# Another order and other engines for attention pairs 0 to 17, weights' sums in halves, part of the norms on VectorE, biases as immediates

## The chip, the cores and the metric

The kernel runs on one core of a Trainium2 chip. The metric is the device time in microseconds of that core, as the median of several runs. Engines are named as in the profile: PE (TensorE, matmuls), DVE (VectorE), ACT (ScalarE), POOL (GpSimd), SP (SyncE, which here only issues DMAs).

## The reference

`q`, `k`, `v` are [8 batches, 12 heads, 448 positions, 64 dimensions] in float32. The result is [3584, 768].

```python
q_n = q / (np.linalg.norm(q, axis=-1, keepdims=True) + 1e-06)
k_n = k / (np.linalg.norm(k, axis=-1, keepdims=True) + 1e-06)
attn = softmax(q_n @ k_n.T / tau)                  # per batch and head, tau = 0.1
x = (attn @ v) with heads side by side             # [3584, 768]
h = x @ w_in                                       # [3584, 2048]
g = h * np.clip(h + 3.0, 0.0, 6.0) / 6.0
out = g @ w_out                                    # [3584, 768]
```

## The kernel before

Two heads make a pair, 48 pairs in all, six to a batch; two pairs make a twin, whose raw `q` and `k` are items `2d` and `2d + 1`. An item is loaded (LQ, two 448 KB tiles of 128 x 896 columns), squared (SQ, on ACT, DVE or POOL, in pieces of columns of 64 if wanted; `SQ.6.v.1.3` is item 6 on DVE, 3 columns from the first), summed (RE, DVE), its reciprocal norms are made (NO: four small ACT operations Ln, Exp, Ln with bias EPS, Exp), and it is normalised (NM, POOL or DVE, into bf16). Then it is transposed: on PE through the identity (TR) for items 0 to 13, by a DMA transpose (XD) from item 14 on. CQ and CK copy a pair's queries and keys out of the transposed tile, CS the last keys; `km` is a copy by POOL for those that came by DMA. For each pair there are four groups of scores (SC), their exponentials (EX, ACT), the products with the values (VA, PE), and the division by the sums (FI, DVE: reciprocal L477, product L478). VC casts the values. BK and CX transpose the result and copy it into `xT`; XP and XB do that by DMA.

When a batch is complete, its MoE units run: 16 `mm1_unit`s (six matmuls, then a relu on ACT, L577, then the product with the bank on DVE, L583, into `gT`), and for batch 0 six `mm2_unit`s (16 matmuls, L615, and a store copied alternately by ACT and DVE). From pair 18 on the second layer uses a scheme with fewer matmuls for blocks of 2 x 2, which needs sums of parts of `w_out` (WS: "1", "6", "7" into `w_sum`, "y3" and "y4" in place; 3072 columns each, L690) and of `gT` (`g_sum`, L719). Outputs of units and scores share a ring of six PSUM banks; before pair 6 scores use two double banks of their own.

Every engine executes its own instructions in the order in which the program issues them, and waits for semaphores of the others. That order is written out by hand: for pairs 0 to 17 in the list `PLAN` (611 tokens, each one step; `U` issues the next MoE unit's matmuls, `UA` and `UV` the oldest outstanding step of a unit on ACT and DVE), and for the rest in loops. `DP.n` and `D.n` are `n` filler matmuls on zeros (`busy_pv`, L923, and `busy`, L918), which compute nothing that is used. `W` lets POOL issue a DMA of one eighth of the weights. `LV` loads a twin's values with four DMAs.

Of the kernel before, what the change touches and what calls it, by code (L numbers as in the profile page):

```python
# [14 lines left out]
EPS = 1e-6  # L15
# [3 lines left out]
ORDER = "111111111111111111111111111111222222"  # L19

PLAN = [
# [36 lines left out]
]  # L58


# [1 line left out]
def kernel(  # L62
# [83 lines left out]
        [const.tile([128, 2, 14], FP32, name=f"{x}{i}", tag=f"{x}{i}") for x in ("ln", "nr", "le", "r")]  # L146
        for i in range(2)
    ]
    bias = const.tile([128, 2], FP32, name="bias", tag="bias")
    eps_bias, half_bias = bias[:, 0:1], bias[:, 1:2]  # L150
    ident = const.tile([128, 128], BF16, name="ident", tag="ident")

    PV = psum.tile([128, 2, 512], FP32, name="PV", tag="PV")
# [92 lines left out]
    def norms(d, *items):  # L246

        needs(("NM", 2 * d - 4), ("NM", 2 * d - 3))
        items = items or (0, 1)
        for x in items:  # L250
            needs(("RE", 2 * d + x))
        it = slice(items[0], items[-1] + 1)
        ln, nr, le, r = (t[:, it, :] for t in rs[d % 2])
        nc.scalar.activation(out=ln, in_=n2s[d % 2][:, it, :], func=AF.Ln)
        nc.scalar.activation(out=nr, in_=ln, func=AF.Exp, scale=0.5)
        nc.scalar.activation(out=le, in_=nr, func=AF.Ln, bias=eps_bias)
        nc.scalar.activation(out=r, in_=le, func=AF.Exp, scale=-1.0)  # L257
        for x in items:
            issued.add(("NO", d, x))

# [301 lines left out]
    def mm1_unit(b, fc):  # L562
# [12 lines left out]
        def relu():  # L575
            u = sb.tile([128, S], BF16, name="u", tag="u", bufs=3)
            nc.scalar.activation(  # L577
                out=u[:, :], in_=ps[:, 0:S], func=AF.Relu, bias=half_bias, scale=1.0 / 6.0
            )
            post["v"].append(lambda: product(u))  # L580

# [90 lines left out]
            return wide[n % 2], wide[2]  # L672
        return wide_late[2 * (n - LOOP) : 2 * (n - LOOP) + 2]

    def weight_sums(what, c0, n):

        w = w_out_sb[:, :, :].rearrange("p (c k) m -> p c k m", k=2)[:, c0 : c0 + n]
        b11, b12, b21, b22 = (w[:, :, k, m] for k in range(2) for m in (LEFT, RIGHT))
        for x in {"y3": "16", "y4": "17"}.get(what, ""):
            assert all((x, c) in summed for c in range(c0, c0 + n))  # L680
        o, x, y, op = {
            "1": (b11, b11, b22, ALU.add),
            "6": (b11, b11, b12, ALU.add),
            "7": (b21, b21, b22, ALU.add),
            "y3": (b12, b12, b22, ALU.subtract),
            "y4": (b21, b21, b11, ALU.subtract),
        }[what]
        if what in w_sum:
            o = w_sum[what][:, c0 : c0 + n, :]
        nc.vector.tensor_tensor(out=o, in0=x, in1=y, op=op)  # L690
        summed.update((what, c) for c in range(c0, c0 + n))

    def half(b, t, k):
# [247 lines left out]
    def whole_units(n, engines="av"):  # L941
# [4 lines left out]
                    finish_units(e)  # L946

    OPS = {
        "LQ": load_qk, "LV": load_v, "W": next_weights, "SQ": square, "RE": reduce, "NO": norms,
        "NM": normalise, "VC": vcast, "TR": transposes, "XD": crossbar, "XB": back_crossbar, "XP": back_two, "CQ": copy_q, "CK": copy_k, "CS": copy_k3, "SC": scores,  # L950
        "EX": exps, "VA": values, "FI": finish_values, "BK": back, "CX": copy_x, "U": unit, "UA": lambda: finish_units("a"), "UV": lambda: finish_units("v"),
        "GL": g_left, "WS": lambda x, *h: weight_sums(str(x), *((h[0] * KC // 2, KC // 2) if h else (0, KC))), "UU": whole_units, "D": busy, "DP": busy_pv, "OPEN": open_ring,
    }

    def do(op, *args):
        OPS[op](*args)
        key = (op,) + tuple(a for a in args if isinstance(a, int))
        if op not in ("RE", "NM", "LQ"):
            issued.add(key[:3] if op == "SC" else key)

    def run(text):
# [7 lines left out]
        nc.vector.memset(t[0:64, 2:4, 0, :], 0.0)  # L969
    zeros = xT[1][:, 0, :]  # L970
    nc.vector.memset(zeros, 0.0)
    nc.vector.memset(eps_bias, EPS)
    nc.vector.memset(half_bias, 0.5)
    make_identity(nc, ident)
    for t in vx:
        nc.vector.memset(t[:, :, D : D + 1], 1.0)
# [120 lines left out]
```

## Time and profile before

| | |
|---|---|
| runs | 405.06, 405.01, 406.67 us; median 405.06 |
| span of the profiled execution (first to last instruction) | 405.6 us; its time outside the span is not recorded |
| granted TensorE clock, mean | 0.998 |
| busy: PE / DVE / ACT / POOL | 396.2 / 288.9 / 278.3 / 233.5 us |
| first filler matmul, first scores, first exponential, first MoE unit | 2.47, 13.66, 14.20, 44.24 us |
| DMA engines' share, 22.4 to 44.2 us | 1.11 (259 GB/s) |

PE's busy time includes fillers, and matmuls overlap, so a busy PE may still have short stalls; the spacing of starts shows them. A line of a timeline gives the start, the length, the engine, the line of the kernel, the operation, what it writes and reads, its shape and how many such instructions were merged, and in brackets the idle time before it and what ended it.

### The profile page before, as it was taken

To read this page: it belongs to the slowest core of one execution; us is meant where nothing else is said; L and a number is where in the kernel's file an instruction comes from. 1 tells how busy PE (TensorE), PEld (TensorE's weight loads), DVE (VectorE), ACT (ScalarE), POOL (GpSimd) and SP (SyncE) were. 2 spreads that over 40 slices of the span, in tenths; PEclk is the share of its full clock that TensorE was granted. 3 is DMA by queue.
4 is the path that set the end of the run, shared out by engine and by line. 5 is a ranking of instruction groups with operands and counts; after the bars stand their busy time and mean duration, and the time that the engine had idled before them with its cause. 6 is when DMAs were issued, how large, how long until landed. Compare 5 with 4: busy or idle time off the path is not lost.

```text
span 405.6 us, 9619 instructions
## 1 busy us (share of the span) xinstructions
PE 396.2 (98%) x3696; PEld 234.5 (58%) x3696; DVE 288.9 (71%) x503; ACT 278.3 (69%) x609; POOL 233.5 (58%) x228
## 2 busy tenths in 40 slices
PE   7899999999989999999999999999999999999996
PEld 4666565555655555655555556556555556555554
DVE  5888777766998777777857887587656666645663
ACT  4899998888467687687767778778757755225230
POOL 6799645761483996587475874886674600410060
PEclk9999999999999999999999999999999999999999
DMA  8899989979988749886799649977964522140134
GB/s 286 251 251 244 236 237 226 184 112 192 223 208 190 184 109 199 200 220 143 172 196 223 132 129 180 184 194 144 188 158 86 112 45 58 40 87 20 24 75 99
DMA packets 91566, 65.32 MB, mean 161 GB/s; under 512 B 56064, under 2 KB 89984, under 8 KB 91520
## 3 DMA queue, kind: packets, MB, share of 16 engines
q1 hardware_dynamic: 87408, 58.02, 62.4%
q0 software_dynamic: 3712, 6.29, 9.0%
q8 instruction: 29, 0.48, 0.5%
q10 hardware_dynamic: 400, 0.39, 0.3%
q14 instruction: 17, 0.14, 0.1%
HBM read 47.19 MB, written 11.01 MB: 143 GB/s over the span
## 4 chain that ended last, share of the span: by engine, by line
PE 91%; DVE 3%; DMA 3%; POOL 1%; SPq 1%; issue 0%; DVEq 0%; POOLq 0%
PE M L568 24%; PE M L741 17%; PE PV L457 13%; PE Y L568 6%; PE M L417 6%; PE Z L568 5%; PE Y L741 4%; PE Z L741 3%; PE M L615 3%; DMA big<-in_q_dram 3%; PE M L821 2%; PE Z L417 2%; PE Z L821 1%; PE Y L417 1%; PE PV L923 1%; PE SC L417 1%
## 5 line engine op out<-in xcount | busy, mean ns | idle before, releaser
L435 ACT ACTIVATE at<-M 128x448 bf16<-128x448 f32 x200 | 99.8, 567 | 16.4 <-PE M L417 14.3
L568 PE MATMUL M<-xT,w_in_sb 128*128 128x448 bf16 x522 | 110.7, 352 | 0.0
L568 PEld LDWEIGHTS <-w_in_sb 128*128 128x128 bf16 x768 | 71.9, 98 | 62.4 <-issue 2.5
L269 POOL TENSOR_TENSOR nrm<-big,r 128x896 bf16<-128x896 f32 (+1 forms) x48 | 79.4, 1658 | 26.0 <-ACT r L257 19.2
L577 ACT ACTIVATE u<-M,bias 128x448 bf16<-128x448 f32 x87 | 57.0, 655 | 26.0 <-PE M L568 25.5
L583 DVE SCALAR_TENSOR_TENSOR gT<-u,M 128x448 bf16<-128x448 bf16 x76 | 46.8, 618 | 38.0 <-ACT u L577 37.3
L226 POOL TENSOR_TENSOR big<-big 128x896 f32<-128x896 f32 (+3 forms) x39 | 63.4, 1628 | 10.0 <-DVE rc L477 5.1
L457 PEld LDWEIGHTS <-at 128*128 128x128 bf16 (+1 forms) x1536 | 54.8, 97 | 24.0 <-issue 14.7
L457 PE MATMUL PV<-vx,at 128*128 128x65 bf16 (+1 forms) x1536 | 64.3, 194 | 0.2 <-DVE on L478 0.2
L238 DVE TENSOR_REDUCE n<-big 128x14 f32<-128x896 f32 (+1 forms) x50 | 51.9, 1041 | 6.2 <-ACT big L224 5.5
L374 POOL COPY km<-tT 64x128 bf16<-64x128 bf16 x34 | 12.7, 372 | 59.6 <-DMA tT<-nrm 44.1
L770 POOL TENSOR_TENSOR big<-big 128x384 f32<-128x384 f32 x11 | 11.8, 1071 | 54.7 <-ACT big L789 54.6
L741 PEld LDWEIGHTS <-gT 128*128 128x128 bf16 x288 | 27.8, 98 | 20.5 <-DVE gT L719 0.8
L741 PE MATMUL M<-w_out_sb,gT 128*128 128x384 bf16 x208 | 37.9, 326 | 0.3 <-DVE gT L719 0.3
L288 POOL CAST vx<-big 128x512 bf16<-128x512 f32 x44 | 33.5, 765 | 3.5 <-DMA big<-in_v_dram 2.4
L435 ACT ACTIVATE at<-Z 128x448 bf16<-128x448 f32 x49 | 27.7, 565 | 9.9 <-PE M L417 7.1
L478 DVE TENSOR_TENSOR on<-PV,rc 128x512 bf16<-128x512 f32 x48 | 33.2, 691 | 1.7
L417 PE MATMUL M<-tT,kz 64*128 64x448 bf16 (+1 forms) x175 | 31.9, 351 | 1.0 <-DVE o L628 1.0
L741 PEld LDWEIGHTS <-gs 128*128 128x128 bf16 x224 | 21.6, 98 | 14.5
L568 PE MATMUL Y<-xT,w_in_sb 128*128 128x448 bf16 x132 | 28.6, 353 | 0.0
L435 ACT ACTIVATE at<-Y 128x448 bf16<-128x448 f32 x45 | 25.7, 570 | 3.1 <-PE Z L417 2.9
L741 PE MATMUL M<-w_sum,gs 128*128 128x384 bf16 x144 | 26.3, 326 | 0.0
(133 smaller groups left out, 565.2 us busy)
## 6 DMA issues: line engine op xcount, KB each, us to landing
big<-in_v_dram SPq DMA_DIRECT2D x96, 128.0 KB, 4.9
big<-in_k_dram SPq DMA_DIRECT2D x24, 448.0 KB, 5.3
big<-in_q_dram SPq DMA_DIRECT2D x24, 448.0 KB, 4.3
out_dram<-o SPq DMA_DIRECT2D x107, 96.0 KB, 2.2
w_in_sb<-in_moe_w_in_dram POOLq DMA_DIRECT2D x4, 768.0 KB, 10.2
w_out_sb<-in_moe_w_out_dram POOLq DMA_DIRECT2D x4, 768.0 KB, 9.1
tT<-nrm SPq DMA_TRANSPOSE x34, 3.4
xT<-on SPq DMA_TRANSPOSE x25, 3.8
```

Source lines behind the costliest of these rows:

```text
L226: engines[e].tensor_tensor(out=o, in0=i, in1=i, op=ALU.mult)
L238: nc.vector.tensor_reduce(out=n2s[d % 2][:, j % 2, c], in_=sq[:, :, :, :].rearrange("p g c d -> p (g c) d")[:, c, :], axis=AX.X, op=ALU.add,)
L269: engines[e].tensor_tensor(out=nrm[:, :, g, :].rearrange("p c g d -> p g c d"), in0=raw_of[j][:, g, :, :], in1=rs[d % 2][3][:, j % 2, :] . ...
L288: (engines[e].copy if e == "a" else engines[e].tensor_copy)(out=o, in_=f)
L417: nc.tensor.matmul(o, ks, qt[rows], start=True, stop=True)
L435: nc.scalar.activation(out=o, in_=x, func=AF.Exp, scale=inv_tau)
L457: nc.tensor.matmul(pv_out(j, h), at[rows, n, q_cols(i // HP, j)], vt[rows, 3 + h if name == "M" else 5 * h + int(name[1]), :], start=(name ...
L478: nc.vector.tensor_tensor(out=on[:, :, :, :].rearrange("p j h d -> p h j d"), in0=pv4[:, :, :, 0:D], in1=rc[:, :, :].to_broadcast([128, 2, ...
L568: nc.tensor.matmul(ps[:, 0:S], w_in_sb[:, cc, fc * 128 : (fc + 1) * 128], x[:, cc, 0:S], start=(cc == 0), stop=(cc == CC - 1),)
L577: nc.scalar.activation(out=u[:, :], in_=ps[:, 0:S], func=AF.Relu, bias=half_bias, scale=1.0 / 6.0)
L583: nc.vector.scalar_tensor_tensor(out=g[:, fc, c0 : c0 + S], in0=u[:, :], scalar=1.0, in1=ps[:, 0:S], op0=ALU.min, op1=ALU.mult,)
L741: nc.tensor.matmul(m, lhs[:, c, :], rhs[:, c, c0 : c0 + width], start=(base is None and c == 0), stop=(c == KC - 1), skip_group_check=True,)
```

## The change

- `PLAN` is another list: 639 tokens, the same steps in another order. The fillers are 86 `DP` and 10 `D` in both, and the units and weights' loads are as many; some steps changed engine, and some squares are now split among engines (items 0 and 1 too, in another way than before). On ACT: new are CQ.1, CQ.6, CQ.10, CX.4, the casts VC.11, 12, 16, 17, square 22 and pieces of 17, 19, 21; gone are squares 15 and 18 and most of 6, 13. On DVE: new are NM.13, NM.14, half of NM.0, VC.9 and pieces of squares 6, 9, 13, 17, 18, 19; gone is square 22. On POOL: new are square 15 and most of 18; gone are pieces of 9, 17, 19, NM.13, NM.14, VC.9, 11, 12, 16, 17 and half of NM.0.
- The weights' sums of `WS` are issued as halves of 1536 columns each, and some earlier in the list.
- For twins 7 and 9 the norms are split: `powers` (NA) makes Ln and Exp on ACT, `reciprocals` (ND) adds EPS and takes the reciprocal on DVE.
- The biases EPS and 0.5 of the activations are immediates; the tile that held them and its two memsets are gone.

Parts of the list (the first lines, two from the middle, the last):

```diff
-    "LQ.1 DP.5 SQ.1.a.11.3 SQ.1.p.4.3 DP.1 SQ.1.a.0.4 LQ.0 SQ.0.p.8.6 DP.2 DP.4 LQ.3 LQ.2 SQ.1.v.7.4 RE.1.1",
-    "SQ.0.a.0.6 RE.1.0 NO.0.1 LQ.5 LQ.4 SQ.0.v.6.2 DP.6 SQ.3.a.0.7 NM.1.p.0 D.10 RE.0.1 DP.3 NM.1.p.1 RE.0.0 DP.8",
-    "NO.0.0 LV.0 DP.2 SQ.2.a.0.7 NM.0.p.0 RE.3 RE.2 NM.0.p.1 TR.1.Y DP.2 TR.0.Z CK.0.v DP.4 SQ.4.p.0.7 CQ.0.v",
+    "DP.1 LQ.1 SQ.1.p.11.2 LQ.0 SQ.0.a.6.2 SQ.1.v.13.1 LQ.3 SQ.1.v.0.4 DP.5 LQ.2 SQ.1.p.7.2 SQ.1.v.9.1 DP.2 DP.8",
+    "SQ.0.p.0.2 SQ.1.v.10.1 SQ.1.a.4.3 RE.1.1 RE.1.0 SQ.0.a.3.1 LQ.5 NO.0.1 NM.1.p.1 DP.4 LQ.4 SQ.0.p.2.1",
+    "SQ.0.v.8.6 DP.4 SQ.0.a.4.2 DP.6 D.10 DP.2 RE.0.1 RE.0.0 SQ.3.a.0.7 DP.3 RE.3 DP.2 NO.0.0 NM.1.p.0 LV.0",
+    "SQ.2.a.0.7 NM.0.p.0 TR.1.Y NM.0.v.1 TR.0.Z CK.0.v RE.2 LV.1 CQ.0.v LQ.6 SQ.4.p.0.7 DP.3 SC.0.0.0 SQ.5.a.0.7",
...
+    "EX.1.1 SQ.7.p.0.7 VA.0.1 NM.5.p DP.5 SC.1.2.0 CK.2.v SQ.6.a.0.1 SQ.6.a.4.1 SQ.6.v.5.2 SQ.6.v.1.3 DP.2",
+    "SC.1.3.1 DP.3 CQ.2.v VA.0.2 VC.3.v EX.1.2 LQ.11 EX.1.3 VA.0.3 DP.2 SC.2.0.0 CK.3.v LQ.10 SC.2.1.1 EX.2.0",
...
-    "SC.13.3 NM.16.p CK.15.v CK.14.v U UA UA SQ.18.a.0.7 EX.13.3 U SC.14.0 FI.12 UA VA.13.0 VC.14.p CS.14.v UV",
-    "VA.13.1 UV EX.14.0 UV U SC.14.1 SC.14.2 VA.13.2 VA.13.3 UA EX.14.1 UV U W SC.14.3 FI.13 U VA.14.0 NM.17.p UA",
+    "NM.16.p U SQ.18.p.1.2 SQ.18.p.3.4 UA FI.12 UV SC.14.0 VC.14.p EX.13.3 UA SC.14.1 VA.13.0 W CS.14.v VA.13.1",
+    "UV EX.14.0 VA.13.2 U UV SC.14.2 VA.13.3 EX.14.1 U SC.14.3 FI.13 VA.14.0 U EX.14.2 UA UA NM.17.p UV XD.17",
...
-    "CK.17.v XD.18 U EX.16.1 SQ.20.a.0.7 NM.19.p FI.15 WS.6 U UV XD.19 SC.16.3 RE.20 GL.0 WS.1 WS.7.0 EX.16.2 U VA.16.0 UA VA.16.1 LV.11",
-    "EX.16.3 SC.17.0 UV VC.19.p SC.17.1 SC.17.2 SQ.22.v.0.7 VA.16.2 LQ.23 EX.17.0 VA.16.3 EX.17.1 LV.10 U SC.17.3",
-    "XP.14 NO.10 FI.16 NM.20.p CK.18.v U CK.19.v WS.7.1 WS.y3 WS.y4.0 XB.16 EX.17.2 UV UA VA.17.0 VC.18.p EX.17.3 RE.22 CS.18.v",
+    "NM.18.v VC.17.a CK.17.v SQ.20.a.0.7 EX.16.1 U RE.21 XD.18 LQ.23 U WS.7.v.0 SC.16.3 VA.15.3 RE.20 WS.6.v.0",
+    "WS.1.v.1 FI.15 XD.19 U VA.16.0 UA EX.16.2 VA.16.1 LV.11 UV EX.16.3 SC.17.0 VC.19.p UV SC.17.1 SC.17.2",
+    "SQ.22.a.0.7 EX.17.0 VA.16.2 EX.17.1 GL.0 VA.16.3 SC.17.3 U LV.10 NO.10 FI.16 NM.20.p EX.17.2 CK.18.v U XP.14",
+    "VA.17.0 WS.y3.v.1 WS.y3.v.0 CS.18.v WS.y4.v.0 UV EX.17.3 WS.7.v.1 CK.19.v XB.16 RE.22 UA VC.18.p",
```

The code:

```diff
-    bias = const.tile([128, 2], FP32, name="bias", tag="bias")
-    eps_bias, half_bias = bias[:, 0:1], bias[:, 1:2]
...
-        nc.scalar.activation(out=le, in_=nr, func=AF.Ln, bias=eps_bias)
+        nc.scalar.activation(out=le, in_=nr, func=AF.Ln, bias=EPS)
...
+    def powers(d, *items):
+        needs(("NM", 2 * d - 4), ("NM", 2 * d - 3))
...
+        nc.scalar.activation(out=ln, in_=n2s[d % 2][:, it, :], func=AF.Ln)
+        nc.scalar.activation(out=nr, in_=ln, func=AF.Exp, scale=0.5)
...
+    def reciprocals(d, *items):
...
+        nc.vector.tensor_scalar_add(out=le, in0=nr, scalar1=EPS)
+        nc.vector.reciprocal(out=r, in_=le)
...
-                out=u[:, :], in_=ps[:, 0:S], func=AF.Relu, bias=half_bias, scale=1.0 / 6.0
+                out=u[:, :], in_=ps[:, 0:S], func=AF.Relu, bias=0.5, scale=1.0 / 6.0
...
-    def weight_sums(what, c0, n):
+    def weight_sums(what, c0, n, e="v"):
...
-        nc.vector.tensor_tensor(out=o, in0=x, in1=y, op=op)
+        engines[e].tensor_tensor(out=o, in0=x, in1=y, op=op)
...
-        "GL": g_left, "WS": lambda x, *h: weight_sums(str(x), *((h[0] * KC // 2, KC // 2) if h else (0, KC))), ...
+        "GL": g_left, "WS": lambda x, e, *h: weight_sums(str(x), *((h[0] * KC // 2, KC // 2) if h else (0, KC)), e), ...
...
-    nc.vector.memset(eps_bias, EPS)
-    nc.vector.memset(half_bias, 0.5)
```

More of the change, by code (lines that the diff above doesn't have):

```diff
@@ L255, in norms @@
         nc.scalar.activation(out=nr, in_=ln, func=AF.Exp, scale=0.5)
-        nc.scalar.activation(out=le, in_=nr, func=AF.Ln, bias=eps_bias)
+        nc.scalar.activation(out=le, in_=nr, func=AF.Ln, bias=EPS)
         nc.scalar.activation(out=r, in_=le, func=AF.Exp, scale=-1.0)
+        for x in items:
+            issued.add(("NO", d, x))
+    def powers(d, *items):
+        needs(("NM", 2 * d - 4), ("NM", 2 * d - 3))
+        items = items or (0, 1)
+        for x in items:
+            needs(("RE", 2 * d + x))
+        it = slice(items[0], items[-1] + 1)
+        ln, nr = (t[:, it, :] for t in rs[d % 2][:2])
+        nc.scalar.activation(out=ln, in_=n2s[d % 2][:, it, :], func=AF.Ln)
+        nc.scalar.activation(out=nr, in_=ln, func=AF.Exp, scale=0.5)
+        for x in items:
+            issued.add(("NA", d, x))
+    def reciprocals(d, *items):
+        items = items or (0, 1)
+        for x in items:
+            needs(("NA", d, x))
+        it = slice(items[0], items[-1] + 1)
+        nr, le, r = (t[:, it, :] for t in rs[d % 2][1:])
+        nc.vector.tensor_scalar_add(out=le, in0=nr, scalar1=EPS)
+        nc.vector.reciprocal(out=r, in_=le)
         for x in items:
@@ L948 @@
     OPS = {
-        "LQ": load_qk, "LV": load_v, "W": next_weights, "SQ": square, "RE": reduce, "NO": norms,
+        "LQ": load_qk, "LV": load_v, "W": next_weights, "SQ": square, "RE": reduce, "NO": norms, "NA": powers, "ND": reciprocals,
         "NM": normalise, "VC": vcast, "TR": transposes, "XD": crossbar, "XB": back_crossbar, "XP": back_two, "CQ": copy_q, "CK": copy_k, "CS": copy_k3, "SC": scores,
         "EX": exps, "VA": values, "FI": finish_values, "BK": back, "CX": copy_x, "U": unit, "UA": lambda: finish_units("a"), "UV": lambda: finish_units("v"),
-        "GL": g_left, "WS": lambda x, *h: weight_sums(str(x), *((h[0] * KC // 2, KC // 2) if h else (0, KC))), "UU": whole_units, "D": busy, "DP": busy_pv, "OPEN": open_ring,
+        "GL": g_left, "WS": lambda x, e, *h: weight_sums(str(x), *((h[0] * KC // 2, KC // 2) if h else (0, KC)), e), "UU": whole_units, "D": busy, "DP": busy_pv, "OPEN": open_ring,
     }
@@ L957, in do @@
         key = (op,) + tuple(a for a in args if isinstance(a, int))
-        if op not in ("RE", "NM", "LQ"):
+        if op not in ("RE", "NM", "LQ", "NA", "ND"):
             issued.add(key[:3] if op == "SC" else key)
```

56 rows, old and new, of the table PLAN are left out of this document.

## The prediction

> **What bounds the kernel now.** I read first the page (busy times, clock), then who waited for whom on TensorE, then the windows by stage, then the timelines of ScalarE and VectorE where TensorE's waits lie.
>
> The page:
>
> ```profile
> PE 396.2 (98%) x3696; PEld 234.5 (58%) x3696; DVE 288.9 (71%) x503; ACT 278.3 (69%) x609; POOL 233.5 (58%) x228
> ```
>
> TensorE is busy for 396.2 of 405.6 us, at the granted clock 1.00 in every window up to 390 us. 13.8 us of it are the fillers of `busy_pv` (L923 x86) and 3.4 us those of `busy` (L918 x10). Both orders hold 86 and 10, so TensorE's work is the same before and after: only its waits can change. The view of who waited (us in total, times, longest) lists nearly all:
>
> ```profile
> PE PV L923 <- DVE vx L976: 2.5, 1, 2.5
> PE Z L314 <- POOL nrm L269: 1.0, 1, 1.0
> PE M L417 <- DVE o L628: 1.0, 1, 1.0
> PE M L741 <- DVE gT L719: 0.3, 1, 0.3
> PE PV L457 <- DVE on L478: 0.2, 1, 0.2
> ```
>
> The first is the start of the program (the two bias memsets that go end at 2.43 us, beside the `zeros` memset's 2.42, so they free nothing). The others make 2.5 us; shorter stalls between matmuls (start to next start, less the usual spacing) add some 1.2 us between 13.7 and 44 us. So no reordering can gain more than about 4 us, 1%, and none of what it speeds up elsewhere is on the path. The windows (length; busy time and instructions of PE, PEld, DVE, ACT, POOL; clock; DMA) show who sets the pace where:
>
> ```profile
> 22.40:44.20 21.80, 21.36 (x325) 14.14 (x325) 19.23 (x50) 21.16 (x44) 20.71 (x18) 1.00 1.11 259
> 44.20:101.50 57.30, 57.30 (x588) 32.94 (x587) 40.99 (x78) 50.42 (x112) 30.12 (x31) 1.00 1.00 192
> 101.50:123.30 21.80, 20.78 (x178) 12.24 (x176) 21.32 (x24) 12.45 (x29) 14.20 (x11) 1.00 0.87 209
> ```
>
> Until 44.2 us it is ScalarE (21.16 of 21.80; GpSimd hardly less); from there TensorE alone; from 101.5 us VectorE (21.32 of 21.80). The hand-over at 44.2, in ScalarE's and TensorE's timelines:
>
> ```profile
> 43.08 1.11 ACT L435 ACTIVATE at<-M 128x448 bf16<-128x448 f32 x2
> 44.24 0.55 PE L568 MATMUL M<-xT,w_in_sb 128*128 128x448 bf16 x2
> ```
>
> The second exponential of the pair is that of SC.8.0's first half; it ends at 44.19. The first MoE unit takes that bank, six allocations later, and starts 0.05 later. So ScalarE's chain from the first exponential (14.20) to this one, 30.0 us with about 0.7 us of idle time in it, sets when the saturated stage begins. Late, in VectorE's timeline (the weights' sums are L690, the store is L628) and TensorE's:
>
> ```profile
> 107.10 2.61 DVE L690 TENSOR_TENSOR w_sum<-w_out_sb 128x3072 bf16<-128x3072 bf16 x2
> 111.50 0.69 DVE L478 TENSOR_TENSOR on<-PV,rc 128x512 bf16<-128x512 f32 x1
> 112.63 0.95 DVE L690 TENSOR_TENSOR w_sum<-w_out_sb 128x1536 bf16<-128x1536 bf16 x1
> 113.50 4.53 DVE L690 TENSOR_TENSOR w_out_sb<-w_out_sb 128x3072 bf16<-128x3072 bf16 x2
> 117.94 0.55 DVE L628 COPY o<-M 128x384 f32<-128x384 f32 x1
> 118.54 0.35 PE L417 MATMUL M<-tT,kz 64*128 64x448 bf16 x1 [1.02 <-DVE o L628]
> 120.62 2.18 DVE L690 TENSOR_TENSOR w_out_sb<-w_out_sb 128x1536 bf16<-128x1536 bf16 x1
> ```
>
> The store of the last unit stands behind 5.5 us of sums, and scores 18.2 wait for its bank. A half (1536 columns) takes 0.95 us at 112.63 and 2.18 at 120.62; at the latter GpSimd runs a normalisation (120.29 to 121.98).
>
> **The change, part by part** (against the execution of 405.6 us; the runs' median is 405.06, and I add the differences to that).
>
> *Up to the first exponential.* Before, ScalarE's square 3 waits for its load (8.76 to 9.71) and norms 0.0 stand behind it; both normalising halves then run on GpSimd (10.73 to 12.56), TR.0 follows at 12.62, and scores 0.0 at 13.66. After, one half goes to VectorE, which could give TR.0 1 us. But CQ.0 now has RE.2 (1.09) ahead of it, and fillers before the first score grow from 37 to 40: CK.0 can begin at about 11.9 (fillers and D.10 end near 11.3, TR.1 takes 0.55), RE.2 at 12.2, CQ.0 (0.39) at 13.3, scores at 13.65. The exponential itself hangs on square 5 (its load lands at 12.36, in the same queue order; 0.95) and NO.1 (0.98; 0.1 less after), which stay: 14.2. If the half on VectorE waits for GpSimd's own half, 0.3 later. Taken: +0.1, from 0 to +0.3.
>
> *ScalarE's chain, 14.2 to 44.2.* Added: CQ.1, CQ.6 (row L334, 0.53, in sequence some 0.44) and CX.4 (0.51, 0.42), together 1.30. Square 6 (19.79 to 20.63, 0.84) becomes two pieces of 128 columns (0.31 each, 0.21 in sequence): -0.42. NO.2 to NO.5 lose the bias read: L256 takes 0.32, its siblings 0.23, so -0.09 each, -0.36. Sum +0.5. Of the 0.7 us idle time 0.46 (EX.2.0 waits for scores, TensorE being full of fillers, which stay 15 between scores 0.3 and 2.0) remains; perhaps 0.2 goes. New: VectorE gets two pieces of square 6 ahead of CQ.2 while GpSimd works without a gap from 17.83 to 24.44. A comparable row is square 0's piece beside GpSimd: 128 columns in 0.62, where 256 took 0.43. Two pieces cost 1 us without that wait and up to 1.7 more each with it; slack before scores 2.0 is about 1.4. Taken +0.5 (0 to 2). The first unit: 44.24 + 0.1 + 0.5 - 0.2 + 0.5 = 45.1, so **+0.9** (0.3 to 2.2). TensorE is saturated afterwards, so this stays to the end.
>
> *44 to 101 us.* The relus' immediate bias (L577 0.655; the same tile without a bias, L435, 0.567) takes 0.09 from each, 11 us of ScalarE over 128, and nothing off the path: TensorE waits nowhere here, and covers it. The same holds for the copies and casts moved among ScalarE, VectorE and GpSimd, and for the norms of twins 7 and 9 (two small VectorE operations for two of 0.3). What is late next: the transposed keys 16. Their DMA is issued at 91.04 behind that of 17 (89.61, waiting for NM.17 on GpSimd), lands at 97.80 and leaves 2.0 us to scores 16.0 (100.13). After, GpSimd has most of square 18 (768 columns, 1.46 like L226's 128x768) and a weight load's issue (0.80) ahead of NM.17: 1.8 to 2.3 later, against 2.0 of slack; LV.8's four loads move ahead of these DMAs, which helps. FI.13 (0.9) is followed by VA.14.0 with a unit (1.13) and a score (0.19) between. Taken **+0.3** (-0.1 to 1.5). In the loop from pair 18 on nothing changes but the relus; the 0.3 at 227 us stays.
>
> *Late, from VA.16.3 (T0, 111.2).* Sums 6, 1 and half of 7 go earlier, square 22 to ScalarE, WS.7.1 and CK.19 behind the store. So the store is ready about 1 us sooner and most of the 1.02 goes. But the same VectorE work still lies between T0 and the product that pair 18 needs: FI.16, two copies, five halves, the store, RE.22, FI.17, product. In the profile that chain takes 12.1 us (to 123.33) without a gap but 0.28; TensorE would need the product at T0 + 10.9. The 1.0 us wait at 118 plus the 0.06 at 123 become 0.3 and 0.9. Five halves cost 7.7 now (0.95, 3.24, 1.36, 2.18). If GpSimd is met once more, as WS.7.1 now falls in its busy stretch: +0.4, **late +0.4** (-1.2 when all are free, 5 x 0.95; +3.2 at 5 x 2.18).
>
> The Trainium skill, "SBUF — State Buffer", section "SBUF: two separate sides", says that VectorE and GpSimd hold a shared port pair as an exclusive lock for a whole instruction. That speaks against cutting sums and squares in pieces: each piece queues for the lock anew. The trace agrees (0.95 against 2.18, as after waiting out a GpSimd instruction); by it alone the sum would be that of the first rival.
>
> Sum: 0.9 + 0.3 + 0.4 = +1.6: 405.06 + 1.6 = **406.7 us**.
>
> **Rivals.**
> 1. *Slower: every piece waits for GpSimd.* The five halves at 2.18 make the late chain 3.2 longer instead of 0.4: 409.5. For it: both sums that met GpSimd's normalising took 1.2 to 1.5 more. Against: GpSimd has gaps. It decides once a half averages over 1.7 us (the forecast has 1.6).
> 2. *Slower: transposed keys 16 land late*, the upper end, 1.5 instead of 0.3: 407.9. It decides when NM.17 ends more than 2 us later. Against: fewer loads beside its DMA.
> 3. *Faster: the pieces fit between GpSimd's instructions.* The late waits (1.1) go and the start costs nothing: 404.0; with the stalls of the first 44 us gone too, 402.3. Against: ScalarE's sum grows.
> 4. *The immediates read no faster.* Then the four norms keep 0.36 us: 407.1. The exponentials without a bias speak against it.
>
> **Numbers.** A measurement of this kernel tells about 0.5% (2.0 us) from no change. Chances: forecast (404.5 to 407.1) 0.48; rival 1 0.19; rival 2 and stalls like it 0.19; rival 3 0.12, of which 0.05 beyond 2 us; rival 4 0.02. Faster: 0.05. Same: 0.48 + 0.07 + 0.02 = 0.57. Slower: 0.38. The likeliest case's own range is 404.5 to 407.1; the 8 in 10 leaves out rival 3 below and, above rival 1's 409.5, its worst: 404.4 to 409.5.
>
> **What would show it.** Right: L577 and L256 near 0.57 and 0.23; first unit near 45; L314's wait of 1.0 gone, but scores 0.0 still near 13.7; the 118 us wait shrunk with a wait on `gT` near 123 in its place; sums' halves at 0.95 to 2.2. Wrong: the first unit at 44 or earlier, no TensorE wait between 110 and 125, or a wait of over 1 us between 45 and 100 that is not at scores 16.

## The result and the profile after

The changed kernel takes 411.23 us (median of 4 runs, 410.40 to 411.60), the kernel before beside it 405.21 us: 6.0 us slower, a ratio of 1.0127 [1.0098, 1.0156]. The prediction was 406.7, with 404.4 to 409.5 as its range.

The profiled execution has a span of 409.5 us and a time of 411.3. The time outside the span, which the profile of before did not give, is 1.7 to 1.9 us in every run that has both. So the execution of before that the prediction was built on (span 405.6) took about 407.4 us (an estimate, 405.6 + 1.8), 2.3 more than the median of its runs. That matters below.

The page's first row of after (busy us, share, instructions):

```profile
PE 396.9 (97%) x3696; PEld 235.4 (57%) x3696; DVE 295.8 (72%) x518; ACT 268.1 (65%) x618; POOL 229.3 (56%) x228
```

TensorE's work is the same 3696 matmuls. ScalarE has 10 us less to do and VectorE 7 us more. Who waited for whom on TensorE (us in total, times, longest):

```profile
PE Z L341 <- POOL nrm L296: 1.6, 1, 1.6
PE SC L444 <- DVE tT L363: 1.3, 3, 0.6
PE PV L484 <- DVE on L505: 1.0, 1, 1.0
PE Z L768 <- DVE gT L610: 0.7, 1, 0.7
PE Y L595 <- DVE gT L610: 0.4, 1, 0.4
...
PE M L444 <- DMA tT<-nrm: 0.2, 1, 0.2
```

The late wait for the store `o` (1.0, the old L628) is no longer there and a wait for `gT` (0.7) is. Keys transposed by DMA, the prediction's suspect between 44 and 101 us, are not waited for there at all: the 0.2 us in the list lies at 181.9 us, in TensorE's timeline

```profile
181.91 0.54 PE L444 MATMUL M<-tT,kz 64*128 64x448 bf16 x3 [0.21 <-DMA tT<-nrm]
```

New or longer are the waits of the scores, of the transposes and of the value products for VectorE and GpSimd, all before 27 us. The wait of the transposes for GpSimd's normalisation, whose 1.0 us the prediction wanted gone, is 1.6. The hand-over, 44.24 us in the first profile of before, is now

```profile
47.28 0.54 PE L595 MATMUL M<-xT,w_in_sb 128*128 128x448 bf16 x2
```

Taking the MoE matmuls of both profiles in order and subtracting their starts gives the delay stage by stage (us, against the profiled execution of before; `e1` to `h1` are experiments below, "before again" is a second profile of the same kernel):

| MoE matmul that before starts at | 44.2 | 95.6 | 113.8 | 119.6 | 124.2 | last |
|---|---|---|---|---|---|---|
| after | +3.04 | +3.54 | +4.20 | +2.98 | +3.63 | +3.88 |
| before again | -1.97 | -1.97 | -1.97 | -1.97 | -2.03 | -2.04 |
| e1, square 6 whole | +0.02 | +0.52 | +1.19 | -0.04 | +0.62 | +0.75 |
| h1, before's order up to the first unit | -0.49 | +0.42 | +1.08 | -0.14 | +0.51 | +0.31 |

Read along a row: three quarters of the delay is there when the first unit starts; 1.2 us come between 44 and 114, 1.2 go at 118 and 0.65 come back at 124. Read the second row against the first: two executions of the same kernel differ by 2 us, nearly all of it (1.9) before the first exponential. Against a usual execution of before, the changed kernel's first unit is 5 us late; it is this line in TensorE's timeline of before again:

```profile
42.27 0.55 PE L568 MATMUL M<-xT,w_in_sb 128*128 128x448 bf16 x2
```

Where it waits, in ScalarE's timeline of after, 21 to 31 us (start, length, idle time and its cause in brackets; before had one gap of 0.46 in this chain):

```profile
22.45 2.54 ACT L462 ACTIVATE at<-SC 128x896 bf16<-128x896 f32 x3 [1.08 <-PE SC L444]
25.57 0.54 ACT L462 ACTIVATE at<-SC 128x448 bf16<-128x448 f32 x1 [0.59 <-PE SC L441]
...
28.62 0.92 ACT L462 ACTIVATE at<-SC 128x896 bf16<-128x896 f32 x1 [0.75 <-PE SC L444]
30.42 1.35 ACT L462 ACTIVATE at<-SC 128x896 bf16<-128x896 f32 x2 [0.89 <-PE SC L444]
```

Scores 2.0 and what follows come late, 3.3 us of gaps in all. What made them late, in VectorE's timeline and in GpSimd's of the same time:

```profile
18.05 3.63 DVE L228 TENSOR_TENSOR big<-big 128x256 f32<-128x256 f32 x2
21.61 0.38 DVE L363 COPY tT<-Z 128x448 bf16<-128x448 bf16 x1
```

```profile
17.77 1.69 POOL L296 TENSOR_TENSOR nrm<-big,r 128x896 bf16<-128x896 f32 x1 [1.59 <-ACT r L259]
19.41 1.86 POOL L228 TENSOR_TENSOR big<-big 128x896 f32<-128x896 f32 x1
21.24 2.00 POOL L296 TENSOR_TENSOR nrm<-big,r 128x896 bf16<-128x896 f32 x1
```

The two pieces of square 6 that the change gives to VectorE stand ahead of CQ.2, the copy at 21.61 that scores 2.0 need. The one of 256 columns takes 1.68 us where a piece of 256 took 0.43 in before, started just ahead of GpSimd's, and the one of 384 takes 2.03 where such a piece took 0.55 with GpSimd idle. The first ends soon after GpSimd's normalisation (19.45), the second soon after its square (21.27): each waited out the rest of an instruction of GpSimd that had started up to 0.3 us before it.

The late chain, in VectorE's timeline (sums are now L717, the store is L655) and TensorE's:

```profile
116.52 4.27 DVE L717 TENSOR_TENSOR w_out_sb<-w_out_sb 128x1536 bf16<-128x1536 bf16 x3
120.91 0.56 DVE L655 COPY o<-M 128x384 f32<-128x384 f32 x1
121.38 1.05 DVE L717 TENSOR_TENSOR w_sum<-w_out_sb 128x1536 bf16<-128x1536 bf16 x1
...
124.44 1.99 DVE L717 TENSOR_TENSOR w_out_sb<-w_out_sb 128x1536 bf16<-128x1536 bf16 x1
126.35 0.61 DVE L610 SCALAR_TENSOR_TENSOR gT<-u,M 128x448 bf16<-128x448 bf16 x1
```

```profile
127.01 0.34 PE L768 MATMUL Z<-w_out_sb,gT 128*128 128x384 bf16 x1 [0.71 <-DVE gT L610]
```

The five halves take 7.3 us (4.27, 1.05, 1.99), the store comes in time, and the product that TensorE needs comes 0.7 late. The relu, in the groups by shape, reads an immediate instead of the tile:

```profile
L604 ACT ACTIVATE u<-M 128x448 bf16<-128x448 f32 x87 | 48.9, 567 | 28.5 <-PE M L595 27.3 <-DVE gT L610 0.6 <-ACT at L462 0.2
```

It takes 567 ns against 655. The Trainium skill, "ScalarE: Activation LUTs", section "What ACT_TABLE_LOAD costs", gives about 93 ns for a pointer operand; the 88 here agree.

### The profile page after: what moved, and what is told of

The parts are those of the page before. It is cut to its first block, busy times and chain, and to the rows that moved or that the text cites. A ratio compares the mean times of both kernels' runs of the same rounds, so it can differ in the third digit from the quotient of the medians.

```text
span 409.5 us, 9658 instructions
## 1 busy us (share of the span) xinstructions
PE 396.9 (97%) x3696; PEld 235.4 (57%) x3696; DVE 295.8 (72%) x518; ACT 268.1 (65%) x618; POOL 229.3 (56%) x228
## 4 chain that ended last, share of the span: by engine, by line
PE 84%; DVE 9%; DMA 2%; ACT 2%; issue 1%; POOL 1%; DVEq 0%; ACTq 0%; POOLq 0%
PE M L595 22%; PE M L768 16%; PE PV L484 11%; PE Y L595 5%; PE M L444 5%; PE Z L595 5%; PE Y L768 4%; PE Z L768 3%; PE M L642 3%; PE M L848 2%; ACT at L462 2%; DVE n L240 2%; PE Z L444 1%; PE Z L848 1%; DVE big L228 1%
## 5 line engine op out<-in xcount | busy, mean ns | idle before, releaser
L296 POOL TENSOR_TENSOR nrm<-big,r 128x896 bf16<-128x896 f32 (+1 forms) x45 | 76.3, 1696 | 31.3 <-ACT r L259 20.1
L228 POOL TENSOR_TENSOR big<-big 128x896 f32<-128x896 f32 (+6 forms) x47 | 66.4, 1418 | 13.9 <-DMA big<-in_k_dram 6.9
L484 PEld LDWEIGHTS <-at 128*128 128x128 bf16 (+1 forms) x1536 | 55.8, 97 | 23.8 <-issue 14.8
L604 ACT ACTIVATE u<-M 128x448 bf16<-128x448 f32 x87 | 48.9, 567 | 28.5 <-PE M L595 27.3
L484 PE MATMUL PV<-vx,at 128*128 128x65 bf16 (+1 forms) x1536 | 65.4, 194 | 1.0 <-DVE on L505 1.0
L401 POOL COPY km<-tT 64x128 bf16<-64x128 bf16 x34 | 14.1, 414 | 59.0 <-DMA tT<-nrm 27.9
L462 ACT ACTIVATE at<-Z 128x448 bf16<-128x448 f32 x51 | 28.9, 567 | 9.0 <-PE M L444 9.0
L595 PE MATMUL Y<-xT,w_in_sb 128*128 128x448 bf16 x138 | 29.9, 352 | 0.4 <-DVE gT L610 0.4
L315 POOL CAST vx<-big 128x512 bf16<-128x512 f32 x39 | 28.2, 727 | 3.1 <-PE PV L484 3.0
```

Of the source, the lines that this page charges most:

```text
L228: engines[e].tensor_tensor(out=o, in0=i, in1=i, op=ALU.mult)
L296: engines[e].tensor_tensor(out=nrm[:, :, g, :].rearrange("p c g d -> p g c d"), in0=raw_of[j][:, g, :, :], in1=rs[d % 2][3][:, j % 2, :] . ...
L315: (engines[e].copy if e == "a" else engines[e].tensor_copy)(out=o, in_=f)
L462: nc.scalar.activation(out=o, in_=x, func=AF.Exp, scale=inv_tau)
L484: nc.tensor.matmul(pv_out(j, h), at[rows, n, q_cols(i // HP, j)], vt[rows, 3 + h if name == "M" else 5 * h + int(name[1]), :], start=(name ...
L595: nc.tensor.matmul(ps[:, 0:S], w_in_sb[:, cc, fc * 128 : (fc + 1) * 128], x[:, cc, 0:S], start=(cc == 0), stop=(cc == CC - 1),)
```

## The experiments

Each was run beside the kernel before on the same chip; "+x" is its median less that of before there. The theory after the first look: the start holds the loss, and square 6's pieces on VectorE are its largest part. Rivals: the part behind the first unit; a half granted clock (3.4 us at 0.5 from about 26 us in the profile of after); the order up to the first exponential.

**e1: square 6 whole on ScalarE again.**

```diff
-... CK.2.v SQ.6.a.0.1 SQ.6.a.4.1 SQ.6.v.5.2 SQ.6.v.1.3 DP.2
+... CK.2.v SQ.6.a.0.7 DP.2
```

> The changed kernel with square 6 whole on ScalarE again (SQ.6.a.0.7), nothing else. Theory A (VectorE's two pieces of square 6 wait for GpSimd's instructions, 1.68 and 2.03 us in the changed kernel's profile, and everything behind them on VectorE is late; TensorE idles and its clock falls to half for 3.4 us): VectorE is some 3.5 us earlier at CQ.2, the clock stays 1.00 after its first rise, the first MoE unit comes at 44.0 to 45.0 instead of 47.3, and the time falls by 2.5 to 4 us, to 407 to 409. Rival B (the start is lost by ScalarE's added copies and the order as a whole): the first unit stays later than 46, and the time falls by less than 1 us.

409.41 us (408.17 to 410.76), +3.7, ratio 1.0097 [1.0072, 1.0123]. The four pieces cost 2.3 us by the two differences to before (6.0 and 3.7). In its profile the first unit starts 3.0 us earlier than in after, and the clock is not halved:

```profile
44.26 0.92 PE L595 MATMUL M<-xT,w_in_sb 128*128 128x448 bf16 x4
```

Behind the first unit its delay grows and shrinks as after's does, within 0.15 us to the end. So more than half of the loss lies elsewhere. (By the traces the pieces cost 2.9 us: from the first exponential to the first unit after takes 33.5 us, e1 30.6.)

**e2: the same four pieces in the kernel before.**

```diff
-... SC.1.2.0 SQ.6.a.0.7 LQ.11 DP.5
+... SC.1.2.0 SQ.6.a.0.1 SQ.6.a.4.1 SQ.6.v.5.2 SQ.6.v.1.3 LQ.11 DP.5
```

> The kernel before with only square 6 in the four pieces of the change (two on ScalarE, two on VectorE) at its old place. Theory A: the two VectorE pieces take 1.5 to 2 us each beside GpSimd's normalisings (NM.4, NM.5), CQ.2 and scores 2.0 come 2 to 3 us later, the first unit at 45.5 to 47.5, and the time grows by 1.5 to 3.5 us. Rival B: the pieces take 0.4 and 0.55 us, the first unit stays within 0.5 us of 44.2, the time within 0.5 us.

406.33 us, +0.6, 1.0033 [1.0008, 1.0058], but three of ten runs took 408.7 to 410.1. The profiled one is of these (408.73). There the pieces took 3.4 us and TensorE stood 1.5 us for the copy behind them, in VectorE's timeline and TensorE's list of waits:

```profile
19.77 3.43 DVE L226 TENSOR_TENSOR big<-big 128x256 f32<-128x256 f32 x2
23.13 0.38 DVE L336 COPY tT<-Z 128x448 bf16<-128x448 bf16 x1
```

```profile
PE SC L417 <- DVE tT L336: 1.8, 2, 1.5
```

So the cost is not fixed. That it depends on what GpSimd is doing when the piece is reached is an inference here, since the fast executions left no trace; g1 below shows it on another piece.

**e3: the kernel before with the immediates alone.**

```diff
-        nc.scalar.activation(out=le, in_=nr, func=AF.Ln, bias=eps_bias)
+        nc.scalar.activation(out=le, in_=nr, func=AF.Ln, bias=EPS)
...
-                ... func=AF.Relu, bias=half_bias, scale=1.0 / 6.0
+                ... func=AF.Relu, bias=0.5, scale=1.0 / 6.0
```

> The kernel before with only the two biases as immediates. Prediction's step: relus 0.567 instead of 0.655 us, the third operation of the norms 0.23 instead of 0.32, first unit earlier by at most 0.4 us, time 0 to 0.4 us less. Rival: a shift of ScalarE's phase moves contention elsewhere and the time changes by over 1 us either way. The span of this run, beside its time, also shows how far the profiled execution of before (405.6) was a usual one: if what lies around the span is 1.8 us as in the changed kernel (411.3 against 409.5), its span is near 403.

405.90 us, +0.2, 1.0012 [0.9992, 1.0032]: no difference. ScalarE has 12 us less to do in its profile and the kernel is not faster; TensorE, not ScalarE, is what is full in the stage of the relus.

**e4: 25 more fillers in the stretch where after's TensorE waited**, so that the clock is not halved.

```diff
-... VA.0.3 DP.2 SC.2.0.0 ... LV.2 TR.4.Y ... LV.3 VA.1.0 ... VA.1.1
+... VA.0.3 DP.9 SC.2.0.0 ... LV.2 DP.5 TR.4.Y ... LV.3 DP.8 VA.1.0 ... VA.1.1 DP.5
```

> The changed kernel with 25 more fillers (2.6 us of matmuls at full clock) where TensorE waited between 21 and 26 us; they compute nothing that is used. If the half clock is a cost of its own (theory A's second part): the clock stays 1.00, the first unit comes 0.5 to 1.5 us earlier (46 to 46.8), time 0.5 to 1.5 us less. If the half clock only fell into time that VectorE's delay cost anyway: the first unit stays at 47.3 and the time within 0.5 us.

410.98 us, +5.3, 1.0142 [1.0125, 1.0160] against after's 1.0127. The clock stays at 1.00 in its profile and the time hardly moves, so the loss does not lie in the half clock. The fillers take TensorE's time too, so a cost of some tenths is not excluded.

**h1: before's order up to SC.8.2 (the first unit), the change's behind it. h2: the reverse, with square 6 whole. h3: the change's order up to the first exponential only, before's behind it.** The edit is the list alone, cut behind the token named; steps done in the first part are left out of the second.

```diff
+h1: before[... SC.8.2]    after[rest]
+h2: after, square 6 whole [... SC.8.2]    before[rest]
+h3: after, square 6 whole [... EX.0.0]    before[rest]
```

> The order of before up to the scores 8.2 ahead of the first MoE unit, then all that is left in the order of the change (with its halves, its norms on VectorE for twins 7 and 9 and its immediates). Theory A2 (the loss is the start; behind the first unit the change costs what the profiles show there, +1.2 us from 57 to 114 us and -0.4 later): 406.2 to 406.8 us. Rival B2 (the later part costs more in the runs than in the profiled execution): 408 us or more.

> The other half: the order of the change up to scores 8.2, with square 6 whole on ScalarE, then what is left in the order of before. Theory A2: the kernel with only square 6 put back has 409.4, of which the part behind the first unit is 0.75; so 408.3 to 409.0. Rival B2: 405.5 to 406.3.

> The order of the change only up to the first exponential (squares and norms of items 0 and 1 in pieces on three engines, half a normalising on VectorE, RE.2 ahead of CQ.0), then that of before. If the beginning itself is slower (the first scores came at 12.5 with the order of before in one profile whose loads were early, at 13.2 to 13.4 with that of the change): 406.4 to 407.5 us. If the loss lies between the first exponential and the first unit (ScalarE's added copies, pieces of square 9, order): within 0.5 us of before.

h1: 406.84 us, +1.3, 1.0021 [1.0000, 1.0043]. h2: 407.87, +2.3, 1.0055 [1.0032, 1.0078]. h3: 407.03, +1.5, 1.0031 [1.0014, 1.0049]. Together h1 and h2 make 3.6, which is e1's 3.7. So the start costs even without square 6's pieces, more than half of that up to the first exponential, and the rest of the list about 1: of h1's 1.3 its profile puts 0.4 at the seam (the delay goes from -0.49 to -0.10 within 13 us of it).

**b_again: the kernel before, profiled a second time**, to see what its start usually is.

> The kernel before once more, for its profile: the span of its runs is 403.1 to 404.7 us in the runs beside the experiments, that of the profiled execution shown was 405.6. Expected: first scores between 12.5 and 13.7 us and the first unit between 42.5 and 44.3, as loads land early or late; behind the first unit the same to 0.1 us.

405.39 us, span 403.6, close to the median of before. TensorE's timeline, and ScalarE's, in which square 3 (6.98) no longer waits for its load:

```profile
11.89 0.56 PE L417 MATMUL SC<-tT,kz 64*128 64x448 bf16 x4
```

```profile
6.98 0.93 ACT L224 ACTIVATE big<-big 128x896 f32<-128x896 f32 x1
7.83 0.22 ACT L254 ACTIVATE ln<-n 128x14 f32<-128x14 f32 x1
...
12.29 0.92 ACT L435 ACTIVATE at<-SC 128x896 bf16<-128x896 f32 x1 [0.33 <-PE SC L417]
```

Norms 0.0 start at 7.83 and the first exponential at 12.29, against 9.62 and 14.20 in the profile that the prediction used; and TensorE's list has no wait for GpSimd's normalisations, which was 1.0 us in the prediction's. After's ScalarE, which does not wait for that load either:

```profile
9.86 0.22 ACT L256 ACTIVATE ln<-n 128x14 f32<-128x14 f32 x1 [0.91 <-DVE n L240]
...
13.78 0.92 ACT L462 ACTIVATE at<-SC 128x896 bf16<-128x896 f32 x1
```

With the change's order norms 0.0 wait for a sum, and the sum for a 64-column piece of square 0 that stands behind a normalisation on GpSimd (VectorE's timeline of after, then GpSimd's):

```profile
9.21 1.61 DVE L240 TENSOR_REDUCE n<-big 128x7 f32<-128x448 f32 x2 [1.17 <-POOL big L228]
```

```profile
7.99 0.94 POOL L296 TENSOR_TENSOR nrm<-big,r 128x448 bf16<-128x448 f32 x1 [1.91 <-ACT r L259]
8.88 0.30 POOL L228 TENSOR_TENSOR big<-big 128x64 f32<-128x64 f32 x1
```

**g1: that piece ahead of the normalisation** (with square 6 whole).

```diff
-... NO.0.1 NM.1.p.1 DP.4 LQ.4 SQ.0.p.2.1 ...
+... NO.0.1 SQ.0.p.2.1 NM.1.p.1 DP.4 LQ.4 ...
```

> The kernel after with square 6 whole on ScalarE (median 409.4), and one token moved: the 64-column piece of square 0 on GpSimd goes ahead of NM.1.p.1 instead of behind it. GpSimd idles from 6.1 to 8.0 us in the trace of after and reaches the piece at 8.88; the sum RE.0.1 waits for it until 9.21, norms 0.0 until 9.86 (7.83 in the second profile of before). Theory (this queue costs the start its 1.5 us): the sum starts near 8.1, norms 0.0 near 9.0 (square 3 stands ahead on ScalarE), first scores near 12.4 instead of 13.2, first unit 0.8 earlier, median 408.4 to 408.8. Rival (the loads' landing sets the first scores, so the order around items 0 and 1 is not it): unchanged, 409.2 to 409.6.

409.65 us, +3.7, 1.0079 [1.0053, 1.0104]: nothing gained, so the theory fails in its numbers. In the profile the sum started at 7.97 as expected, but square 3 stood ahead of the norms on ScalarE and waited for a late load (8.86), and the first scores came at 13.79. The trace showed something else instead. The three lines are VectorE's piece of square 9 (512 columns; before has square 9 whole on GpSimd) in e1, in g1 and in h2:

```profile
27.33 0.87 DVE L228 TENSOR_TENSOR big<-big 128x512 f32<-128x512 f32 x1
```

```profile
28.82 2.20 DVE L228 TENSOR_TENSOR big<-big 128x512 f32<-128x512 f32 x1
```

```profile
27.67 2.50 DVE L226 TENSOR_TENSOR big<-big 128x512 f32<-128x512 f32 x1
```

One instruction, three lengths. In e1 GpSimd's normalisation ended 0.3 us into the piece (27.64) and GpSimd then waited for a load; in g1 and h2 a square was under way on GpSimd, in GpSimd's timeline of g1 this one:

```profile
28.80 1.68 POOL L228 TENSOR_TENSOR big<-big 128x896 f32<-128x896 f32 x1
```

and VectorE's piece ended 0.54 after it (31.02 and 30.48). The norms behind the piece waited on ScalarE, in g1:

```profile
32.25 0.23 ACT L256 ACTIVATE ln<-n 128x28 f32<-128x28 f32 x1 [1.31 <-DVE n L240]
```

**g4: squares 6 and 9 both whole, as before. g5: g4 with g1's edit.**

```diff
-... SQ.9.p.6.1 ... SQ.9.p.4.2 ... SQ.9.v.0.4 NM.6.p
+... SQ.9.p.0.7 ... NM.6.p
```

> The kernel after with square 6 whole on ScalarE and square 9 whole on GpSimd, as before (the change puts 512 of its 896 columns on VectorE). That piece took 0.68 us in the profile of after and 0.87 in e1, where GpSimd had just stopped, but 2.20 in g1 and 2.50 in h2, where a square of GpSimd ran beside it; there ScalarE's norms waited 1.31 and 1.60 us for the sum behind it. Theory (VectorE's square pieces beside GpSimd are the start's second loss, in most executions though not in all profiles): no wait of ScalarE over 0.5 near 31 us, median 0.7 to 1.3 under e1's and g1's 409.4 to 409.7, at 408.2 to 408.9. Rival (GpSimd, with 0.9 us more of square 9 ahead of normalisation 6, is late instead, or the piece rarely collides): 409.2 to 410.

> As g4_sq6_sq9_whole, with the 64-column piece of square 0 on GpSimd ahead of NM.1.p.1 (the edit of g1). Theory (in g1 what the earlier start won was given back at square 9's piece and at loads that landed 2 us later in the profiled execution): first scores 0.8 earlier than g4's where the loads are early, median 0.3 to 0.8 under g4's. Rival (the loads set the first scores in most executions): as g4, within 0.3.

g4: 408.33 us, +2.6, 1.0060 [1.0044, 1.0075], 1.1 less than e1 (+3.7). g5: 408.89, +3.1, 1.0073 [1.0056, 1.0090], 0.6 less than g1. The wait of the norms is gone in g5's profile, where the early part is otherwise as in g1:

```profile
31.16 0.22 ACT L255 ACTIVATE ln<-n 128x28 f32<-128x28 f32 x1
```

The intervals of e1 and g4 still overlap a little; the mechanism is shown by the traces, its size in the medians is about 1 us. g1's edit gains nothing here either. In both its profiles the third load came late (square 3 at 8.86 and 9.06), so what it does with early loads was not seen.

**g2: the late part alone (the change's list from FI.14 on). g3: the middle alone (from the first unit to FI.14).** Both with before's list elsewhere and with the immediates.

```diff
+g2: before[... FI.14]    after[rest]
+g3: before[... SC.8.2]    after[... FI.14]    before[rest]
```

> Before's order to FI.14 (about 99 us), the change's list behind it (sums in halves, square 22 on ScalarE, norms of twin 9 split), biases as immediates throughout. Theory (from the trace of after): the 1.0 us wait for o at 118 us goes (matmuls 1.2 earlier behind it), a wait for gT of 0.65 comes at 126: 0.5 under before, 404.7 to 405.1, ratio 0.998 to 0.999. Rival (the prediction's sum): +0.4, 405.8; rival 1 of the prediction (every half waits for GpSimd): +3, over 408.

> Before's order to SC.8.2 (first MoE unit) and again from FI.14 on, the change's list between, biases as immediates. Theory: TensorE is saturated there, and the change's list visits the 64-row score groups three times more (each change to or from 64 rows costs 0.1 us in both traces, a visit 0.2) and issues SC.13.0 before its exponential has freed the bank (0.5): +1.1, 406.3 to 406.8. Rival (VectorE's and ScalarE's steps, not the visits, made the 1.1 in the whole change, as they were late from the start): 405.2 to 405.7, no wait at SC.13.0. Rival 2 of the prediction (transposed keys 16 late): a wait of up to 1.5 at scores 16.0.

The kernel before beside these two and g1 took 405.93 us in the median, but 407.4 to 409.5 in eight of 28 runs, and the ratios count these too. g2: 407.30 us, 1.0025 [0.9995, 1.0055]. Behind 113.8 us its profile does what after's does: matmuls 1.2 earlier where the wait for `o` was, 0.65 later at the wait for `gT`. But where the two lists are joined it loses 0.9 at scores 16 (98.9 and 99.6 us, for an exponential and for a store by ScalarE), which neither whole list has, and half of its runs lie near 406, half near 408.3, so its time says nothing of the late part. g3: 406.93, 1.0009 [0.9982, 1.0035]: its delay grows by 1.0 at the join (matmuls at 48.5 and 50.7 us wait for `gT`), then by 0.9 up to 113.8 us, where after's grows by 1.2 in all. Hybrids of two lists pay at the seam, so these two are inconclusive in their times.

## Why the prediction was wrong

Against a usual execution of before, by the medians: square 6's pieces 2.3 (after less e1), square 9's about 1.1 (e1 less g4), the order to the first exponential 1.5 (h3), ScalarE's longer chain 0.6 (e1's trace), and all behind the first unit 0.9 (h1 without its seam; 0.84 in after's profile). That makes 6.4 for 6.0 measured. The prediction had 0.5, nothing, 0.1, 0.3 and 0.7.

The parts are less certain than their good sum looks. h2 measures the start without square 6's pieces at 2.3, where the terms above make 3.2. And after's profiled execution (411.3) against that of before again (405.4) closes without square 9, whose piece took 0.68 there: 1.5 us to the first exponential, 3.5 from there to the first unit (33.5 against 30.0, of which 2.9 go in e1's profile, where square 6 is whole) and 0.9 behind it. So square 9's loss is seen in executions like those of g1 and h2; that it is part of after's 6.0 is not shown.

- **Square 6's pieces: the term was mis-sized.** The prediction wrote "Two pieces cost 1 us without that wait and up to 1.7 more each with it; slack before scores 2.0 is about 1.4. Taken +0.5 (0 to 2)". The price with the wait held (3.63 us for both, where 1 + 2 x 1.7 is at most 4.4). The choice between the ends did not: GpSimd was known to work "without a gap from 17.83 to 24.44", so both pieces were likely to meet it, and 1 + 2 x 1.7 - 1.4 is 3.0, over the upper end given; measured are 2.3 by the medians and 2.9 by the traces. Both pieces met it in after, in e4 and in e2's profile; what they met in e2's seven faster runs, 405.8 to 406.8, is not known. Rival 1 was this mechanism, and the late sums were its only place; it had to be applied to every piece. The rule of the exclusive lock that the prediction quotes (the Trainium skill, "SBUF — State Buffer", section "SBUF: two separate sides") was the right guide here: in after, e2, e4, g1 and h2 each delayed piece of squares 6 and 9 ends 0.3 to 0.6 us after an instruction of GpSimd.
- **Square 9's piece was not costed at all**, though the change lists it. It meets GpSimd in some executions (2.20 in g1, 2.50 in h2) and hardly in others (0.68 in after, 0.87 in e1), so that its cost in after's runs is open.
- **The first exponential: the forecast was near by luck, its reference was wrong.** It was predicted at 14.2 + 0.1 and came at 13.78. But 14.20 was the value of an execution 2.3 us over the median, whose late loads hid 1.5 us of the new order's cost; the sum then added the difference to the median. The step that failed is "the runs' median is 405.06, and I add the differences to that": a difference in the very stretch in which the profiled execution was untypical can't be added to the median. Which instruction of the new order holds the 1.5 stays open: the piece on GpSimd is what the trace of after names, and moving it ahead (g1, g5) gained nothing. The half normalisation on VectorE, hoped to bring TR.0 forward by 1 us, ran beside GpSimd's half, which took 1.38 us where the one at 7.99 took 0.94:

```profile
10.89 1.38 POOL L296 TENSOR_TENSOR nrm<-big,r 128x448 bf16<-128x448 f32 x1 [0.82 <-ACT r L259]
```

- **ScalarE's sum was about right.** From the first exponential to the first unit before takes 30.0 us (both profiles) and e1 30.6; for a whole square 6 the prediction's terms (1.30 - 0.36 - 0.2) give 0.7.
- **44 to 101 us: wrong place.** Predicted 0.3 at the transposed keys 16 and FI.13; 1.2 came by 114 us. Counted in the traces, TensorE changes from 128-row to 64-row matmuls 19 times in after and 16 times in before, between the first unit and the matmul that before starts at 113.8 us. Between matmuls of 448 columns a start comes 0.28 to 0.29 us after the last one at such a change, in either direction, instead of 0.19: 0.1 each way, so three more visits cost 0.6 (an estimate; no run has the visits alone). In before's timeline 73.25 to 73.44 is a step without a change, 75.81 to 76.10 one from 64 rows back to 128:

```profile
73.25 0.35 PE L417 MATMUL Z<-tT,kz 128*128 128x448 bf16 x1
73.44 2.43 PE L568 MATMUL M<-xT,w_in_sb 128*128 128x448 bf16 x12
75.81 0.36 PE L417 MATMUL M<-tT,kz 64*128 64x448 bf16 x2
76.10 1.31 PE L568 MATMUL Y<-xT,w_in_sb 128*128 128x448 bf16 x6
```

The wait for `gT` at 79.6 us, in after's timeline, adds 0.41:

```profile
79.62 0.35 PE L595 MATMUL Y<-xT,w_in_sb 128*128 128x448 bf16 x1 [0.41 <-DVE gT L610]
```

The visits stand in the lists and their price in the trace of before, so this term could have been worked out. The Trainium skill, "TensorEngine Tiling (Array Packing)", section "Key Properties", says that changing the tiling mode drains TensorE; the 0.1 us agrees with that.
- **Late: right in mechanism, wrong in sign.** The 1.02 us wait left the store and a smaller one (0.71 for a predicted 0.9) came at the product; the halves averaged 1.46 for a predicted 1.6, under the 1.7 at which rival 1 decides. Net -0.57 in after's profile from 113.8 to 124.2 us (4.20 to 3.63), where +0.4 was taken. That the 0.7 predicted for all behind the first unit lies near the 0.9 is luck: 0.3 for 1.2, and +0.4 for -0.57.
- **The immediates** read 88 ns faster, as predicted, and changed nothing that the runs can tell (e3); the 0.36 that the prediction gave them in the norms of the start is below what they resolve.
- **The range.** Its upper end, 409.5, was set by rival 1 at the late sums alone, with the start at +0.9. The start's own upper end, 2.2, is less than its terms make (0.3 + 0.5 - 0.2 + 2 = 2.6). With rival 1's mechanism at the pieces too (3.0 instead of 0.5) the upper end would have been 412.0, above the result.

No version beat the kernel before: with the immediates alone (e3) it is equal to it.

## What to carry to other kernels

A piece of elementwise work moved to VectorE beside a busy GpSimd must be priced at up to its own length plus a whole instruction of GpSimd, each piece anew (in h2 it was slightly more), and all of it falls on what stands behind it in VectorE's queue: here 0.97 us of work took 3.63 and held up a 0.38 us copy that the critical scores needed. Before a difference is added to a median, see whether the profiled execution is a typical one in that stretch, by its time against the runs' and by where it waits for loads. And where a saturated engine's order changes, count its changes of mode as well as its instructions.

## What was not expected of the hardware

- The same VectorE square of 512 columns took 0.68, 0.87, 1.66 (e4), 2.20 and 2.50 us. A delayed piece ended at the same distance behind GpSimd's instruction each time: 0.28 us for the 256 columns (after, e2, e4), 0.41 for the 384 (the same three), 0.54 to 0.56 for the 512 (e1, e4, g1, h2), each some 0.13 less than it took alone (0.43, 0.55, 0.68). In h2 it lost twice in a row: to a normalisation of GpSimd that ended at 27.98 and to the square that followed it (27.94 to 29.61), though VectorE's piece starts at 27.67 in the trace, before that square. GpSimd itself lost far less, 2.00 for a normalisation of 1.69.
- The third load of the program landed 2 us later in some executions of either order (square 3 starts at 6.98 or 8.76 in before and at 8.86 in g1, there when the load lands; at 8.02 in after ScalarE was busy until then), with these loads issued within 0.1 us of the same times. The cause was not found.
- A half granted clock of 3.4 us around 26 us, in an execution with TensorE waits of 0.5 to 1.0, cost nothing that fillers could win back (e4).
